# Where the float64 weight pieces of a second MoE are converted: eight or twelve of sixteen during the first MoE

## The chip, the cores and the metric
One core of a Trainium2 chip. The metric is the device time of one execution in microseconds (us); the kernel of before has a median of 831.95 us over 3 runs (831.78 to 834.63).

## What is computed
Attention with a banded mask, then a top-1 mixture of experts (first MoE), then a dense feed-forward with softplus (second MoE). What matters here:

```
# first MoE, N = 2304 tokens, D = 512, 8 experts, F = 1024
for e in range(8):
    h = np.maximum(x[mask_e] @ w1[e], 0.0)
    out[mask_e] = gate_w[mask_e] * eom[mask_e, e] * (h @ w2[e])
# second MoE
h = x @ w_in                                           # 512 x 2048
g = np.maximum(h, 0.0) + np.log1p(np.exp(-np.abs(h)))
out = g @ w_out                                        # 2048 x 512
```

`w_in` and `w_out` arrive as float64. The engines here compute in float32, so the kernel loads the 64-bit words and puts each float32 together from their two halves with shifts and masks.

## The kernel before
**Numbers.** Every product is taken in three matmuls (`mm3`, L836): each float32 operand is split into a high part (a cast, on ScalarE) and a low part (a subtraction), and hi x hi, hi x lo and lo x hi are summed in PSUM. A weight piece is 128 x 1024 numbers, 512 KB. `hi_` (L1008) casts a piece on ScalarE (L756), `lo_` (L1011) subtracts (L701) on VectorE or on GpSimd: in the first MoE the odd pieces go to GpSimd, in the second all pieces from 8 on.

**First MoE.** The loop at L1266 goes over eight experts in order of load, called ranks, with 424 columns (tokens) in rank 0 down to 256 in rank 7 (`CAPS`, L36). A rank has 16 units `u` of twelve matmuls: units 0 to 7 are `up` (L845), 8 to 15 `down` (L868). `up` writes one of three PSUM buffers (`ph`); ScalarE's ReLU (hh, L852) and VectorE (hl, L853) read it, and only then is it free. In an even unit one piece is cast, in the odd unit after it its low part is subtracted: units 0 to 7 do pieces 4 to 7 of the rank itself, units 8 to 15 pieces 0 to 3 of the next. So piece 5 is cast in unit 2 and subtracted from unit 3, piece 7 in units 6 and 7. The next rank's tokens are transposed on TensorE in units 7, 8 and 9 (L824), with two PSUM buffers (`px`); ScalarE (xh) and VectorE (xl, L701 with px as input) read them one and two units later. The third transposition therefore waits for the first xl. Engines take their instructions in the order of the program; GpSimd's order alone is left to the scheduler.

**Conversion ahead of time (prep).** `PREP` (L146) lists the tiles of 128 x 512 float64 numbers that are converted during the first MoE: 16 of them make the eight pieces below `DIRECT` (L144). `prep_tick` (L191) runs in units 0, 5, 10 and 15 of every rank from 1 on (L1311) until the list is done. One tick finishes a tile (`prep_move`: three VectorE operations at L170, L172 and L174, then a store of 256 KB to HBM on SP's queue), loads a tile four ahead (512 KB, SP's queue), and starts the next (`prep_abs` on ScalarE, L160, `prep_clamp` on VectorE, L164). The ready pieces are loaded back later like other weights (L743). All weights pass through `RB` = 5 buffers (L25); `load_next` (L992) is called when a low part is done, so that a load stands five pieces ahead of its cast.

**Second MoE.** Six blocks of 384 tokens by 16 parts of the hidden layer make 96 steps (L1398), the first 32 of them alternating between two blocks, so that the 16 pieces are needed one after another: pieces 8 to 11 from step 16 on, 12 to 15 from step 24 on. A step is twelve matmuls of `gemm1` (pg, L839 to L841) and nine of `gemm2` (q, L1378 to L1380), which lags three steps (`LAG`, L1400); the first three steps are `gemm1` alone. Softplus is made of three functions (L1342 to L1364): ScalarE's Abs, Exp, Ln (L1355) and ReLU and the cast gh (L1364), VectorE's L1349, L1351, L1356, L1358 and the low part gl (L701). In a step they come in the order c of two steps ago, a of this one, b of the last. The first two of three matmuls of `gemm2` read gh, the third (L1380) reads gl.

**Conversion in place (direct).** Pieces from `DIRECT` on are loaded as float64 in two halves (L726) and converted by `direct` (L765) in four parts at steps `D_AT + D_STEP * (j - DIRECT) + D_OFF`: Abs of each half on ScalarE; eight VectorE operations, set between those of softplus by `aside` (L760); two casts of half a piece (L785); and two half subtractions on GpSimd. `N_HL` (L29) gives the units at which ready pieces are cast, counted from rank 7's start: 16 is step 0 of the second MoE. The subtraction comes one unit later.

Of the kernel before, what the change touches and what calls it, by code (L numbers as in the profile page):

```python
# [25 lines left out]
WARM = 28  # L26
NE_AT = ((6, 14), (7, 0), (7, 1), (7, 2))
X2_AT, X2_HL = (0, 3), ((4, 5, 6, 7), (10, 11, 12, 13))
N_HL = (3, 5, 7, 9, 11, 13, 15, 16)  # L29

D_AT, D_STEP, D_OFF = 2, 3, (0, 1, 3, 4)
XG = 6
IDX_AT, GATHER_AT = 8, 12
TR_AT = (5, 7, 8, 9)
# [6 lines left out]
def attn_moe_softplus_kernel(ctx: ExitStack, tc: tile.TileContext, q, k, v, w_gate, w_ogate, w1, w2, w_in, w_out, out, dbg=None):  # L41
# [99 lines left out]
    PC = 512  # L141


    DIRECT = 8  # L144
    N_IN, N_OUT = DIRECT // 4, DIRECT // 4 * (PC // P)
    PREP = [(0, r_, c_) for r_ in range(DM // P) for c_ in range(N_IN)] + [(1, r_, 0) for r_ in range(N_OUT)]  # L146
    NPREP = len(PREP)
# [557 lines left out]
    def load_idx(r, row0, n):  # L705
        nt = (n + P - 1) // P
        t = K["ixe" if r == 0 else "ix"].tile([P, nt, 2], I32, name=f"idx{r}")
        (nc.gpsimd if r == 0 else nc.sync).dma_start(t, idx_dram[ds(row0, nt * P)].rearrange("(t p) c -> p t c", p=P))
        idx[r] = t
# [6 lines left out]
    def load_piece(r, j, e=None):  # L716
        if r == NE and j >= DIRECT:

            pieces[r, j] = []
            for h in range(2):  # L720
                if j % 2 == 0:
                    src = w_in.bitcast(I32)[256 * h : 256 * h + 256, 256 * j : 256 * j + 512].rearrange("(c p) f -> p c f", p=P)
                else:
                    src = w_out.bitcast(I32)[128 * (j - 1 + h) : 128 * (j - 1 + h) + 128].unsqueeze(1)
                t = K["wr"].tile([P, 1024], F32, tag="wr", name=f"wr{r}_{j}{h}").bitcast(I32)
                nc.sync.dma_start(t.rearrange("p (c f) -> p c f", c=src.shape[1]), src)  # L726
                pieces[r, j].append(t)
            return
        if r == NE:
            g = j // 2  # L730
            if j % 2 == 0:
                src = w_in32[:, 256 * g : 256 * g + 256].rearrange("(c p) f -> p c f", p=P)
            else:
                src = w_out32[256 * g : 256 * g + 256].rearrange("(c p) d -> p c d", p=P)
        elif j < 4:
            src = w1[ds(e, 1), :, 256 * j : 256 * j + 256].rearrange("o (c p) f -> p (o c) f", p=P)
        else:
            src = w2[ds(e, 1), 256 * (j - 4) : 256 * (j - 3)].rearrange("o (c p) d -> p (o c) d", p=P)
        if r == "v" or r == NE and j < 4:
            raw_ = K["wa"].tile([P, 1024], F32R, tag="wa", name=f"wr{r}_{j}").bitcast(F32)  # L740
        else:
            raw_ = K["wr"].tile([P, 1024], F32, tag="wr", name=f"wr{r}_{j}")
        nc.sync.dma_start(raw_.rearrange("p (c f) -> p c f", c=src.shape[1]), src)  # L743
        pieces[r, j] = [raw_]
# [55 lines left out]
    def ntile(n):  # L800
        return (n + P - 1) // P

    def gather(r, n, t):
        rows = min(P, n - P * t)
        xg[r, t] = x_ = K["xge" if r == 0 else "xg"].tile([P, DM], F32, tag="xg", name=f"xg{r}_{t}")
        return nc.gpsimd.indirect_dma_start(
            out=x_[:rows],
            out_offset=None,
            in_=x_dram[: NL0 if r == 0 else NT],
            in_offset=IndirectOffsetOnAxis(ap=idx[r][:rows, t, 0:1], axis=0),  # L810
        )
# [174 lines left out]
    def tab_load(eng, i, m):  # L986
        return eng.value_load(tabi[0:1, i : i + 1], min_val=0, max_val=m)
# [4 lines left out]
    def load_next():  # L992

        nload[1] += 1
        while nload[1] and nload[0] < len(order_):
            r, j = order_[nload[0]]
            two = r == NE and j >= DIRECT
            if two and nload[1] < 2:
                break
            if r not in er and r != NE:  # L1000
                if not K.get("ranked"):
                    break
                er[r] = tab_load(nc.sync, r, NE - 1)
            load_piece(r, j, er.get(r))
            nload[0] += 1
            nload[1] -= 1 + two
# [219 lines left out]
    def x2_load(b):  # L1226
        for h in range(2):
            if b < 2:
                t = new_b("x2r", 2 * b + h).bitcast(F32)[:, : 2 * BT]
            else:  # L1230
                t = K["wr"].tile([P, 1024], F32, tag="wr", name=f"x2r{b}{h}")[:, : 2 * BT]
            x2[b, h] = t = t.rearrange("p (c t) -> p c t", c=2)
            ld = nc.sync.dma_start(t, yT_dram[256 * h : 256 * h + 256, BT * b : BT * b + BT].rearrange("(c p) t -> p c t", p=P))


            begin = [0] + [NP // NE + (r - 1) * ((NT - NP // NE) // (NE - 1)) for r in range(1, NE)]
            need = max(r for r in range(NE) if begin[r] < BT * (b + 1))
            x2_read.append((need, ld))
            for o in range(2 * h, 2 * h + 2):
                tc.add_manual_dep(  # L1240
                    ld.ins,
                    ywr[need, o].ins.name,
                    mybir.DependencyInfo(mybir.DependencyClass.Sync, mybir.DependencyReason.DATA),
                    reason="the last rank whose columns may be read",
                )
                for r in range(need + 1, NE):
                    if (r, o) in ywr:
                        tc.declare_no_dep(ld.ins, ywr[r, o].ins, reason="later ranks lie behind these columns")
# [10 lines left out]

    for j, u in enumerate(N_HL):  # L1260
        last_rank.setdefault(u, []).append((hi_, NE, j))
# [4 lines left out]
    for r in range(NE):  # L1266
        n = CAPS[r]
        if r == 1:
            sched.close()
            overflow()  # L1270
            mctx.enter_context(tc.manual_schedule(engines=manual))
        off = tab_load(nc.scalar, NE + r, NT) if r else 0
        perm_off = tab_load(nc.sync, NE + r, NT) if r else 0
        nc.sync.dma_start(perm_dram[ds(perm_off, NT)], idx_dram[ds(er[r] * NT, NT)])
        for u in range(16):

            if r == 0:
                next(ordering, 0)
                if u == 4:
                    K["ranked"] = True  # L1280
                    er[1] = tab_load(nc.sync, 1, NE - 1)
                    load_idx(1, er[1] * NT, CAPS[1])
                    nload[1] -= 1
                    load_next()
            if r + 2 < NE:
                if u == IDX_AT:
                    if r + 2 not in er:
                        er[r + 2] = tab_load(nc.sync, r + 2, NE - 1)
                    load_idx(r + 2, er[r + 2] * NT, CAPS[r + 2])
                if 0 <= u - GATHER_AT < ntile(CAPS[r + 2]):  # L1290
                    gather(r + 2, CAPS[r + 2], u - GATHER_AT)
            if r + 1 < NE:
                m = CAPS[r + 1]
                if r == 0 and 0 <= u - 6 < ntile(m):
                    gather(r + 1, m, u - 6)
                for s, fn in zip((9, 10, 11, 12) if r == 0 else TR_AT, (gather_scale, gather_tr, gather_hi, gather_lo)):
                    if 0 <= u - s < ntile(m):
                        fn(r + 1, m, u - s)

            if r < NE - 1 or u < 8:  # L1300
                k_ = (r, 4 + u // 2) if u < 8 else (r + 1, (u - 8) // 2)
                (hi_, lo_)[u % 2](*k_)
            if r == NE - 1:
                for fn, *a in last_rank.get(u, ()):
                    fn(*a)
            if (r, u) in NE_AT:
                load_piece(NE, NE_AT.index((r, u)))
            if r == NE - 1:
                if u in X2_AT:
                    x2_load(X2_AT.index(u))  # L1310
            if r and u % 5 == 0:  # L1311
                prep_tick(new_b, NPREP, 3)
            if u < 8:
                up(r, n, u)
            else:
                down(r, n, (u - 8) // 2, u % 2, off, nc.scalar)
# [93 lines left out]
    for b in range(2, NB):  # L1410
        s0 = NF * (b - 1)
        x2_at(b, *((s0 + 8, s0 + 12, s0 + 13, s0 + 13, s0 + 14) if b == 2 else (s0 + 4, s0 + 8, s0 + 9, s0 + 10, s0 + 11)))
    for j in range(DIRECT, NF):
        for s in range(4):
            post.setdefault(D_AT + D_STEP * (j - DIRECT) + D_OFF[s], []).append((direct, j, s))
    for i in range(len(steps) + LAG):
# [54 lines left out]
```

## Time and profile before

| | |
|---|---|
| median of 3 runs | 831.95 us (831.78 to 834.63) |
| the profiled execution | 839.03 us |
| its span, first to last instruction | 837.5 us |
| mean granted TensorE clock | 0.981 |
| TensorE matmul, busy | 784.0 us (94%) |
| VectorE, busy | 551.9 us (66%) |
| ScalarE, busy | 473.7 us (57%) |
| GpSimd, busy | 199.7 us (24%) |
| DMA moved | 104.17 MB |

Attention lies ahead of 173.5 us, the first MoE between 173.5 and 420.8 us, the second from 420.8 us on. A row in order of time gives the start in us, the duration in us, the engine, the line, the operation with output <- input and shapes, and in brackets the idle time before it with what ended it. PE is TensorE, DVE VectorE, ACT ScalarE, POOL GpSimd. Matmuls overlap, so a matmul's duration is longer than the distance to the next; distances between starts are what counts.

### The profile page before, as it was taken

To read this page: it belongs to the slowest core of one execution; us is meant where nothing else is said; L and a number is where in the kernel's file an instruction comes from. 1 tells how busy PE (TensorE), PEld (TensorE's weight loads), DVE (VectorE), ACT (ScalarE), POOL (GpSimd) and SP (SyncE) were. 2 spreads that over 40 slices of the span, in tenths; PEclk is the share of its full clock that TensorE was granted. 3 is DMA by queue.
4 is the path that set the end of the run, shared out by engine and by line. 5 is a ranking of instruction groups with operands and counts; after the bars stand their busy time and mean duration, and the time that the engine had idled before them with its cause. 6 is when DMAs were issued, how large, how long until landed. Compare 5 with 4: busy or idle time off the path is not lost.

```text
span 837.5 us, 14769 instructions
## 1 busy us (share of the span) xinstructions
PE 784.0 (94%) x5542; PEld 701.9 (84%) x5543; DVE 551.9 (66%) x1079; ACT 473.7 (57%) x912; POOL 199.7 (24%) x173
## 2 busy tenths in 40 slices
PE   6788877799999999999899999999999999999995
PEld 5566645599999999999898878899999999999994
DVE  5467757474366776743778989886656665666653
ACT  3575633354546556655667566665655655655553
POOL 9501032435242454543202121211001001001001
PEclk9899989899999999999999999999999999999998
DMA  9979755418779889777832222221001001001000
GB/s 205 260 172 173 140 142 157 132 27 251 229 240 282 291 267 299 229 221 210 273 107 66 87 81 64 76 76 38 20 1 38 1 1 38 1 0 39 1 1 38
DMA packets 88844, 104.17 MB, mean 124 GB/s; under 512 B 31004, under 2 KB 65180, under 8 KB 88768
## 3 DMA queue, kind: packets, MB, share of 16 engines
q1 hardware_dynamic: 78688, 87.50, 38.3%
q0 software_dynamic: 3888, 10.12, 3.6%
q10 hardware_dynamic: 6192, 5.56, 2.0%
q8 instruction: 45, 0.74, 0.4%
q14 instruction: 31, 0.25, 0.1%
HBM read 83.98 MB, written 19.32 MB: 123 GB/s over the span
## 4 chain that ended last, share of the span: by engine, by line
PE 46%; issue 16%; DVE 6%; ACT 3%; POOL 1%; DMA 1%; SPq 0%; POOLq 0%; DVEq 0%
PE q L1380 4%; PE pg L840 4%; PE pg L841 4%; PE pg L839 4%; PE q L1378 4%; PE q L1379 4%; PE ph L839 3%; PE ph L841 3%; PE ph L840 3%; PE py L839 3%; PE py L840 3%; PE py L841 3%; DVE l L1358 1%; DVE gl L701 1%; ACT gh L1364 1%
## 5 line engine op out<-in xcount | busy, mean ns | idle before, releaser
L701 POOL TENSOR_TENSOR wl<-wr,wh 128x1024 fp32r<-128x1024 f32 (+1 forms) x46 | 99.5, 2170 | 204.0 <-ACT wh L785 108.3
L840 PE MATMUL pg<-xlm,wh 128*128 128x384 f32 x384 | 129.6, 338 | 0.0
L839 PE MATMUL pg<-xhm,wh 128*128 128x384 f32 x384 | 129.4, 337 | 0.0
L841 PE MATMUL pg<-xhm,wl 128*128 128x384 f32 x384 | 129.4, 337 | 0.0
L1380 PE MATMUL q<-wh,gl 128*128 128x512 f32 x288 | 114.0, 396 | 2.2 <-DVE gl L701 2.1
L1378 PE MATMUL q<-wh,gh 128*128 128x512 f32 x288 | 113.9, 396 | 0.4
L1379 PE MATMUL q<-wl,gh 128*128 128x512 f32 x288 | 113.1, 393 | 0.0
L1364 ACT CAST gh<-l 128x384 fp32r<-128x384 f32 x96 | 49.2, 512 | 99.9 <-DVE l L1358 99.9
L756 ACT CAST wh<-wr 128x1024 fp32r<-128x1024 f32 x72 | 75.2, 1049 | 16.2 <-ACT y L862 7.3
L701 DVE TENSOR_TENSOR gl<-l,gh 128x384 fp32r<-128x384 f32 x96 | 57.1, 595 | 41.0 <-ACT gh L1364 38.1
L839 PE MATMUL ph<-xh,wh 128*128 128x424 f32 (+7 forms) x256 | 80.7, 315 | 3.1 <-DVE hl L853 2.4
L1387 POOL DMA_INDIRECT out_dram<-o,perm_sb x18 | 18.6, 1035 | 271.9 <-DVE o L251 137.5
L839 PE MATMUL py<-hh,wh 128*128 128x424 f32 (+7 forms) x256 | 81.8, 320 | 0.0
L840 PE MATMUL py<-hl,wh 128*128 128x424 f32 (+7 forms) x256 | 80.7, 315 | 0.8 <-DVE hl L853 0.8
L841 PE MATMUL py<-hh,wl 128*128 128x424 f32 (+7 forms) x256 | 80.5, 314 | 0.0
L841 PE MATMUL ph<-xh,wl 128*128 128x424 f32 (+7 forms) x256 | 80.3, 314 | 0.0
L840 PE MATMUL ph<-xl,wh 128*128 128x424 f32 (+7 forms) x256 | 80.2, 313 | 0.0
L839 PEld LDWEIGHTS pg<-xhm,wh 128*128 128x128 f32 x384 | 72.1, 188 | 3.9
L701 DVE TENSOR_TENSOR wl<-wr,wh 128x1024 fp32r<-128x1024 f32 x42 | 61.9, 1478 | 20.4 <-ACT wh L756 14.1
L840 PEld LDWEIGHTS pg<-xlm,wh 128*128 128x128 f32 x384 | 72.1, 188 | 3.9
L841 PEld LDWEIGHTS pg<-xhm,wl 128*128 128x128 f32 x384 | 72.1, 188 | 0.0
L1349 DVE TENSOR_SCALAR w<-u 128x384 f32<-128x384 f32 x96 | 34.7, 362 | 56.4 <-ACT u L1347 55.6
(193 smaller groups left out, 1656.0 us busy)
## 6 DMA issues: line engine op xcount, KB each, us to landing
wr<-in_moe_w_dram SPq DMA_DIRECT2D x64, 512.0 KB
raw<-in_q_dram SPq DMA_DIRECT2D x8, 576.0 KB
raw<-in_k_dram SPq DMA_DIRECT2D x8, 576.0 KB
x2r<-yT_dram SPq DMA_DIRECT2D x12, 384.0 KB
vP<-in_v_dram SPq DMA_DIRECT2D x16, 272.0 KB
praw<-in_moe_w_in_dram SPq DMA_DIRECT2D x8, 512.0 KB
praw<-in_moe_w_out_dram SPq DMA_DIRECT2D x8, 512.0 KB
wr<-in_moe_w_in_dram SPq DMA_DIRECT2D x8, 512.0 KB
```

The source lines that it names most:

```text
L701: e.tensor_tensor(lo, src, hi.bitcast(F32), ALU.subtract)
L756: (eng or nc.scalar.copy)(d[1], d[0])
L839: nc.tensor.matmul(ps, wh, xh, start=(first and i == 0), stop=False)
L840: nc.tensor.matmul(ps, wh, xl, start=False, stop=False)
L841: nc.tensor.matmul(ps, wl, xh, start=False, stop=(last and i == k - 1))
L1349: nc.vector.tensor_scalar(w_, u, 1.0, None, ALU.add)
L1358: nc.vector.tensor_tensor(l, l, u, ALU.subtract)
L1364: nc.scalar.copy(gT[b, f][0], l)
L1378: nc.tensor.matmul(acc[b, t], gh[:, ts_], wh, start=(f == 0), stop=False)
L1379: nc.tensor.matmul(acc[b, t], gh[:, ts_], wl, start=False, stop=False)
L1380: nc.tensor.matmul(acc[b, t], gl[:, ts_], wh, start=False, stop=(f == NF - 1))
L1387: sc = nc.gpsimd.indirect_dma_start(out=out, out_offset=IndirectOffsetOnAxis(ap=perm_sb[:, b * (BT // P) + t, 0:1], axis=0), in_=o, in_off ...
```

## The change
Twelve pieces instead of eight are converted during the first MoE (24 tiles instead of 16), with five ticks in a rank, in units 0, 3, 6, 9 and 13. Pieces 8 to 11 become ready pieces, cast in units 18, 21, 24 and 27, which are steps 2, 5, 8 and 11 of the second MoE, and subtracted on GpSimd one step later. The four pieces 12 to 15 are still converted in place, the first at step 4, five steps apart.

```
-N_HL = (3, 5, 7, 9, 11, 13, 15, 16)
+N_HL = (3, 5, 7, 9, 11, 13, 15, 16, 18, 21, 24, 27)

-D_AT, D_STEP, D_OFF = 2, 3, (0, 1, 3, 4)
+D_AT, D_STEP, D_OFF = 4, 5, (0, 1, 3, 4)
...
-    DIRECT = 8
+    DIRECT = 12
     N_IN, N_OUT = DIRECT // 4, DIRECT // 4 * (PC // P)
...
-            if r and u % 5 == 0:
+            if r and u in (0, 3, 6, 9, 13):
                 prep_tick(new_b, NPREP, 3)
```

## Rows read from the trace of the kernel before

**Rows 1.** The table by stretch: rank 3, rank 4, and the second MoE with conversions.
```profile
core 0: us, PE busy (x) PEld busy (x) DVE busy (x) ACT busy (x) POOL busy (x), PEclk, DMA share, GB/s
281.00:311.30 30.30, 30.30 (x206) 30.01 (x205) 21.95 (x32) 18.36 (x30) 13.01 (x8) 1.00 0.92 289
311.30:340.30 29.00, 29.00 (x205) 28.77 (x204) 21.14 (x33) 18.10 (x30) 14.26 (x8) 1.00 0.87 281
...
455.00:545.00 90.00, 87.41 (x420) 73.69 (x419) 80.91 (x150) 60.47 (x130) 20.30 (x14) 1.00 0.26 75
```

**Rows 2.** TensorE in order of time, second MoE (start us, us, operation).
```profile
429.65 0.39 PE L1380 MATMUL q<-wh,gl 128*128 128x512 f32 x1
...
431.28 0.34 PE L839 MATMUL pg<-xhm,wh 128*128 128x384 f32 x1
...
443.88 0.34 PE L839 MATMUL pg<-xhm,wh 128*128 128x384 f32 x1
...
470.38 0.34 PE L839 MATMUL pg<-xhm,wh 128*128 128x384 f32 x1
...
537.94 0.34 PE L839 MATMUL pg<-xhm,wh 128*128 128x384 f32 x1
```

**Rows 3.** VectorE in order of time, second MoE.
```profile
427.76 0.56 DVE L1358 TENSOR_TENSOR l<-l,u 128x384 f32<-128x384 f32 x1
428.89 0.56 DVE L701 TENSOR_TENSOR gl<-l,gh 128x384 fp32r<-128x384 f32 x1 [0.58 <-ACT gh L1364]
...
432.44 0.56 DVE L701 TENSOR_TENSOR gl<-l,gh 128x384 fp32r<-128x384 f32 x1 [0.58 <-ACT gh L1364]
...
443.40 1.67 DVE L1358 TENSOR_TENSOR l<-l,u 128x384 f32<-128x384 f32 x1
```

**Rows 4.** ScalarE in order of time, second MoE.
```profile
426.54 0.51 ACT L1355 ACTIVATE w<-w 128x384 f32<-128x384 f32 x1
```

**Rows 5.** GpSimd in order of time, second MoE.
```profile
443.34 2.90 POOL L701 TENSOR_TENSOR wl<-wr,wh 128x512 fp32r<-128x512 f32 x2 [34.02 <-ACT wh L785]
```

**Rows 6.** Groups by line and shape, VectorE, 420.8 to 545 us.
```profile
L172 DVE SCALAR_TENSOR_TENSOR wr<-wr,cm 128x512 int32<-128x512 int32 x16 | 10.9, 683 | 0.0
...
L164 DVE TENSOR_SCALAR cm<-cm 128x512 f32<-128x512 f32 x16 | 6.7, 418 | 0.0
```

**Rows 7.** The page, part 5: costliest groups, the casts of weight pieces.
```profile
L756 ACT CAST wh<-wr 128x1024 fp32r<-128x1024 f32 x72 | 75.2, 1049 | 16.2 <-ACT y L862 7.3
```

**Rows 8.** GpSimd in order of time, ranks 3 and 5 of the first MoE.
```profile
294.03 2.62 POOL L701 TENSOR_TENSOR wl<-wr,wh 128x1024 fp32r<-128x1024 f32 x1 [5.06 <-ACT wh L756]
...
305.88 2.42 POOL L701 TENSOR_TENSOR wl<-wr,wh 128x1024 fp32r<-128x1024 f32 x1
...
345.21 2.97 POOL L701 TENSOR_TENSOR wl<-wr,wh 128x1024 fp32r<-128x1024 f32 x1 [3.35 <-ACT wh L756]
352.08 2.47 POOL L701 TENSOR_TENSOR wl<-wr,wh 128x1024 fp32r<-128x1024 f32 x1 [3.91 <-ACT wh L756]
```

**Rows 9.** VectorE in order of time, ranks 3 and 4 of the first MoE.
```profile
291.05 1.22 DVE L701 TENSOR_TENSOR wl<-wr,wh 128x1024 fp32r<-128x1024 f32 x1
...
294.31 0.90 DVE L853 SCALAR_TENSOR_TENSOR hl<-ph,hh 128x328 fp32r<-128x328 f32 x2
...
296.96 0.69 DVE L701 TENSOR_TENSOR xl<-px,xh 128x512 fp32r<-128x512 f32 x1
...
306.16 3.24 DVE L701 TENSOR_TENSOR wl<-wr,wh 128x1024 fp32r<-128x1024 f32 x1 [2.06 <-issue]
...
339.98 2.17 DVE L164 TENSOR_SCALAR pw<-pw 128x512 f32<-128x512 f32 x1 [0.57 <-ACT pw L160]
```

**Rows 10.** TensorE in order of time, ranks 3 and 5 of the first MoE.
```profile
298.14 0.45 PE L824 MATMUL px<-identf,xg 56*128 56x56 f32 x4
...
349.85 0.29 PE L839 MATMUL ph<-xh,wh 128*128 128x288 f32 x1
...
355.59 0.42 PE L824 MATMUL px<-identf,xg 24*128 24x24 f32 x4
```

## The prediction, made before the change was run

> **What bounds it.** First I read the table by stretch, to see which engine is full where. In ranks 3 and 4 of the first MoE TensorE is busy throughout and its granted clock is 1.00, the 2.4 GHz level; where the second MoE converts pieces (455 to 545 us) it is busy 87.41 of 90 us, and VectorE there 80.91 [rows 1]. So two questions decide: what this stretch loses, and whether the ranks, which lose nothing to VectorE now, stay so.
>
> Second, the matmuls by time. Three undisturbed steps take 443.88 - 431.28 = 12.60 us, 4.20 each. Between 470.38 and 537.94 lie fifteen steps, 13.51 per three [rows 2]: each piece, three steps apart, makes TensorE wait 0.91 us. Seven pieces pay that and the first about half: 7.5 x 0.91 = **6.8 us**, all that the second MoE has to give.
>
> Third, the softplus operations by time, for the cause. In an undisturbed stretch one gl follows the other by 432.44 - 428.89 = 3.55 us [rows 3]: ScalarE and VectorE run a loop that is 0.65 us shorter than a step. A piece therefore adds 13.51 - 3 x 3.55 = 2.86 us to the loop, against 1.95 that three steps have to spare. Part of that are its eight VectorE operations (0.42 to 0.68 us each [rows 6]). The rest is GpSimd: its two half subtractions run from 443.34 [rows 5], and the VectorE operation that starts at 443.40 takes 1.67 us in place of 0.56 [rows 3]. A VectorE operation on SBUF waits until the GpSimd subtraction ends. The first MoE shows it for a whole piece: GpSimd starts at 305.88, VectorE's own subtraction, 1.22 us when free as at 291.05, takes from 306.16 to 309.40 [rows 8, 9], so it began at about 308.15 and was held for **2.27 us** from GpSimd's start. The clamp, one of the operations of a tick, is held as well (2.17 us at 339.98 [rows 9], 0.42 when free [rows 6]).
>
> **The change, second MoE.** Removed: pieces 8 to 11 as direct conversions, 4 x 2.86 us of loop. The other four stand five steps apart: 5 x 0.65 = 3.25 us to spare against 2.86, so by themselves they cost nothing. Added: pieces 8 to 11 as ready ones, a cast on ScalarE and a subtraction on GpSimd each, at steps 2/3, 5/6, 8/9 and 11/12. The cast takes 1.05 us [rows 7] and fits between Ln, which ends at 426.54 + 0.51 = 427.05 [rows 4], and the next gh, which waits for L1358 to end at 428.32 [rows 3]: nothing. The subtraction is not free. Ready at 428.1, it starts when that L1358 ends, 428.32, and holds VectorE to 430.6; gl, due at 428.89, comes **1.7 us late**. The first matmul that reads gl stands at 429.65, and gl ends at 429.45 [rows 2, 3]: 0.2 us of margin, because the four opening steps are shorter than the loop.
>
> Sum over steps 3 to 13: four subtractions 4 x 1.7 = 6.8, two direct pieces (12 and 13) 5.7, together 12.5 us; to spare are 0.2 + 10 x 0.65 = 6.7. TensorE waits **5.8 us**, in place of 6.8: a gain of 1.0. The price of a whole subtraction beside the loop has no row: if VectorE's idle 0.4 us ahead of its next operation absorbs part, 1.3 each, the waits are 4.2; if a whole hold lands on the loop, 2.27 each, 8.1. So the second MoE gives between -2.6 and +1.3 us; I take -1.0, as the hold falls right before gl.
>
> **The change, first MoE.** Eight more tiles are prepared: eight loads, eight Abs on ScalarE, 8 x 4 VectorE operations (2.2 us a tick), eight stores, and later four loads of ready pieces for eight half loads of raw ones. By count the work reaches the first unit of rank 6 instead of rank 5's second tick. VectorE has room in sum (21.95 of 30.3 us in rank 3 [rows 1]); the place is what costs. The tick of unit 5 stood ahead of the GpSimd subtraction of piece 7; the tick of unit 6 meets it in every rank, since its cast is issued in unit 6. In rank 3 that subtraction starts at 294.03 [rows 8]; whichever goes first, hold, last move and clamp must all pass before the two hl behind them: 294.03 + 2.27 + 0.69 + 0.42 = 297.4. Then two hl (0.90) and xl (0.69) [rows 9], overlapping by 0.1: 298.9. The third transposition, which needs the PSUM buffer that this xl reads, stands at 298.14 [rows 10]: TensorE waits **0.8 us**. Rank 5, with units 12% shorter: 352.08 + 3.38 + 1.4 = 356.85 against 355.59 [rows 8, 10], 1.25. On this line ranks 1, 2 and 4 give 0.4, 0.6 and 1.0; in all 4.05.
>
> The tick of unit 3 meets the subtraction of piece 5 where units are short. In rank 5 that ends at 345.21 + 2.97 = 348.18 [rows 8]; two moves, clamp and hl follow, 0.69 + 0.69 + 0.42 + 0.45 less 0.1 of overlap, to 350.3, and unit 6, which needs the PSUM buffer, stands at 349.85 [rows 10]: 0.5 us. If the first, shifting operation is held too, 0.9. With half as much in rank 4, 0.75 to 1.35; I take 1.1, nearer the held end, since the clamp, of the same kind and length, is held. The Trainium skill says the same of the operation that no row shows: by SBUF — State Buffer, Who interferes with whom, a one-input VectorE operation of this kind can take both ports and is then locked out by GpSimd for a whole instruction; by that the wait would be 1.35. First MoE: **+5.15 us**.
>
> What hides the rest: the Abs goes into ScalarE's idle time (18.36 of 30.3 us busy in rank 3 [rows 1]). SP's stores wait for the last move and stand ahead of weight loads, but those run five buffers ahead, and the casts' idle time ends with ScalarE's own work, not with a load [rows 7]; without that cover each late move would be a late cast. DMA is the tight one. Rank 4 moved 281 GB/s x 29.0 us = 8.15 MB at a share of 0.87, which is 323 GB/s at full share [rows 1]; by the count it gets three loads (512 KB) and one store (256 KB) more, some 1.83 MB, and needs 30.9 us, 1.9 over. Bounds 0 and 1.9; I take 0, as the ranks lengthen by 1 to 2 us themselves. The Trainium skill, DMA: Bandwidth & Descriptors, Specifications, gives about 358 GB/s for a core's HBM; by that the estimate is 27.9 us and no loss at all.
>
> Sum: +5.15 - 1.0 = +4.15, on the profiled execution 839.03 to 843.2, on the median 831.95 to **836.1 us**. The profiled one is 0.9% above the median and used for differences only.
>
> **Rivals.** 1, faster: the holds miss. If GpSimd's subtractions in the second MoE fall into gaps of VectorE, or gl has more margin than 0.2 us, and the ticks cost 1 us in all, the 6.8 us go and the time is 826.2. For it: no rank has a wait on VectorE today. Against: the cast fixes the phase of the hold, at each of the four pieces alike. 2, slower: at the start of ranks 5 and 6 VectorE is still at the tick of the unit before (rank 6 gets one for the first time) and GpSimd's piece 5 is ready first; then VectorE's own subtraction of piece 4 and the hl behind it wait a full hold, 2.27 us a rank, 840.6. It decides when piece 5's cast ends before VectorE reaches piece 4. 3: the DMA excess of rank 4 delays weights by 1.9 us: 838.0. 4: the moved work is hidden (first MoE +0.5) and the second keeps its 5.8 us of waits: 831.5. That the change doesn't do what it says I see no way for: the counts follow from the constants.
>
> **Numbers.** My forecast has 0.50, rival 1 0.20, rival 2 0.16, rival 3 0.06, rival 4 0.08. A measurement here tells about 0.5% (4.16 us) from no change, and the forecast lies on that line: half of it counts as slower, half as the same. Slower: 0.25 + 0.16 + 0.04 = 0.45; faster: 0.17 of rival 1; same: 0.38. The range runs from rival 1 to rival 2 with the DMA excess: 826 to 842; the forecast's own is 833 to 839.
>
> **What would show it.** Right: VectorE's gl at about 430.6 behind a GpSimd subtraction and a wait near 1.5 us of TensorE at step 3; no waits after step 14; in ranks 2 to 5 a wait of TensorE for VectorE's xl ahead of the third transposition, longer in later ranks. Wrong: 4.2 us steps throughout from 431 on; ranks 1 to 6 as long as now; a ScalarE cast waiting for a load.

## The result, and the profile after

The changed kernel has a median of 843.77 us (840.34 to 848.83, 4 runs) against 833.29 us (831.78 to 835.34, 4 runs) for the kernel before: a ratio of 1.0133, 95% interval [1.0088, 1.0177]. It is slower, as the prediction had it as likeliest, but by 10.5 us in place of 4, and lies above the range (826 to 842).

The profiled execution took 848.83 us, its span is 847.3 us, 9.8 more than before. The stages split that by the starts of their first matmuls. The first MoE takes 431.09 - 172.66 = 258.43 us, **11.1 more**; the second 416.2 us to the end of the span, 0.5 less; what lies ahead of them 0.8 less.

The table by stretch, after: ranks 2 to 6 of the first MoE, then the whole second MoE (columns as in [rows 1]).
```profile
250.29:282.18 31.89, 31.50 (x206) 31.18 (x205) 27.58 (x36) 19.18 (x31) 11.99 (x8) 1.00 0.92 297
282.18:315.14 32.96, 30.87 (x206) 29.98 (x205) 28.68 (x36) 19.02 (x31) 13.40 (x8) 1.00 0.92 300
315.14:347.21 32.07, 29.57 (x206) 28.84 (x205) 27.95 (x36) 18.67 (x31) 12.48 (x8) 1.00 0.86 281
347.21:377.93 30.72, 27.44 (x206) 26.70 (x205) 26.95 (x38) 18.30 (x31) 12.42 (x7) 1.00 0.82 275
377.93:403.47 25.54, 25.54 (x202) 25.54 (x201) 12.89 (x18) 14.79 (x24) 9.88 (x5) 1.00 0.76 224
431.09:847.30 416.21, 403.74 (x2018) 364.68 (x2016) 281.12 (x531) 242.99 (x519) 40.22 (x30) 0.99 0.11 33
```
Rank 3 took 30.30 us with TensorE idle in none of them [rows 1]; now it takes 32.96 with 2.1 us idle, and VectorE's share rises from 21.95 of 30.30 to 28.68 of 32.96. The granted clock is 1.00 in all of these ranks, so the loss is waiting and not pace. Rank 6, where the work has ended, has no wait at all.

For whom TensorE waits is in the groups by line of the first MoE (173.5:420.8 before, 172.66:431.09 after; the last column is the idle time ahead of the group and what ended it). Before:
```profile
L839 PE MATMUL ph<-xh,wh 128*128 128x424 f32 (+7 forms) x256 | 80.7, 315 | 3.1 <-DVE hl L853 2.4 <-PEq L1192 0.5 <-issue 0.2
L824 PE MATMUL px<-identf,xg 128*128 128x128 f32 (+6 forms) x84 | 11.6, 259 | 0.6 <-issue 0.4 <-DVE xl L701 0.2
```
After:
```profile
L839 PE MATMUL ph<-xh,wh 128*128 128x424 f32 (+7 forms) x256 | 81.8, 320 | 8.0 <-DVE hl L853 7.3 <-PEq L1192 0.4 <-issue 0.2
L824 PE MATMUL px<-identf,xg 128*128 128x128 f32 (+6 forms) x84 | 11.7, 261 | 4.4 <-DVE xl L701 4.2 <-ACT xg L815 0.2
```
Two waits, then: 4.0 us more for xl (the third transposition) and 4.9 more for hl (a PSUM buffer of `up`). By distances between matmul starts, less the usual distance, the first is 1.36, 0.62, 0.59, 0.81 and 1.24 us in ranks 1 to 5, together 4.6; the second stands ahead of units 3 and 4 of ranks 3, 4 and 5, 1.89, 1.91 and 2.44, together 6.2. The two make 10.8 of the 11.1 us.

**The wait for hl**, at the start of rank 4 (315.14 us). VectorE, GpSimd and TensorE in order of time, after:
```profile
310.06 3.33 DVE L701 TENSOR_TENSOR wl<-wr,wh 128x1024 fp32r<-128x1024 f32 x1 [3.91 <-ACT wh L756]
313.31 0.41 DVE L170 TENSOR_SCALAR pw<-pw 128x512 int32<-128x512 int32 x1
313.76 2.92 DVE L172 SCALAR_TENSOR_TENSOR pw<-praw,pw 128x512 int32<-128x512 int32 x1
...
319.57 0.42 DVE L164 TENSOR_SCALAR pw<-pw 128x512 f32<-128x512 f32 x1
...
320.30 3.42 DVE L701 TENSOR_TENSOR wl<-wr,wh 128x1024 fp32r<-128x1024 f32 x1
323.65 0.86 DVE L853 SCALAR_TENSOR_TENSOR hl<-ph,hh 128x312 fp32r<-128x312 f32 x2
```
```profile
309.87 2.43 POOL L701 TENSOR_TENSOR wl<-wr,wh 128x1024 fp32r<-128x1024 f32 x1
313.73 2.40 POOL L701 TENSOR_TENSOR wl<-wr,wh 128x1024 fp32r<-128x1024 f32 x1 [1.44 <-ACT wh L756]
320.26 2.38 POOL L701 TENSOR_TENSOR wl<-wr,wh 128x1024 fp32r<-128x1024 f32 x1 [4.13 <-ACT wh L756]
```
```profile
324.17 0.41 PE L839 MATMUL ph<-xh,wh 128*128 128x312 f32 x1 [1.75 <-DVE hl L853]
```
Read it from the top. GpSimd's piece 1 (309.87) holds VectorE's piece 2; the tick of unit 13 comes behind it and runs into GpSimd's piece 3 (313.73: the move at 313.76 takes 2.92 us in place of 0.69). The tick of unit 0 follows without a pause until 319.99, and one hl behind it. So VectorE comes to piece 4 at 320.30, when GpSimd has taken piece 5 at 320.26: 0.04 us too late, and a whole hold. In the kernel before, the same two instructions stood the other way round, by 0.19 us:
```profile
310.50 2.78 DVE L174 SCALAR_TENSOR_TENSOR pw<-praw,pw 128x512 int32<-128x512 int32 x1
...
316.18 1.21 DVE L701 TENSOR_TENSOR wl<-wr,wh 128x1024 fp32r<-128x1024 f32 x1
```
```profile
309.92 2.81 POOL L701 TENSOR_TENSOR wl<-wr,wh 128x1024 fp32r<-128x1024 f32 x1 [1.61 <-ACT wh L756]
316.37 3.29 POOL L701 TENSOR_TENSOR wl<-wr,wh 128x1024 fp32r<-128x1024 f32 x1 [3.64 <-ACT wh L756]
```
The chain itself is therefore not new: there too piece 3 (309.92) holds the last tick of the rank before (310.50), with the tick of unit 0 behind it. What is new is when VectorE comes out of it. Counted from the rank's first matmul, GpSimd starts piece 5 of rank 4 after 5.12 us in both kernels, and VectorE comes to piece 4 after 4.93 us before and 5.16 after. In ranks 3 and 5 it was 0.73 and 0.52 us ahead of GpSimd, and is now 0.35 and 0.55 behind.

**The wait for xl**, later in the same rank, after: the tick of unit 6, whose last move is held by GpSimd's piece 7, and behind it two hl and xl.
```profile
330.03 2.90 DVE L174 SCALAR_TENSOR_TENSOR pw<-praw,pw 128x512 int32<-128x512 int32 x1
...
333.97 0.67 DVE L701 TENSOR_TENSOR xl<-px,xh 128x512 fp32r<-128x512 f32 x1
```
```profile
330.00 2.38 POOL L701 TENSOR_TENSOR wl<-wr,wh 128x1024 fp32r<-128x1024 f32 x1 [7.36 <-ACT wh L756]
```
```profile
334.70 0.43 PE L824 MATMUL px<-identf,xg 32*128 32x32 f32 x4 [0.74 <-DVE xl L701]
```

**The second MoE** keeps its waits in other places. Distances between steps of 4.20 us grow at steps 3, 9, 10, 12 and 13 by 1.46, 0.50, 1.06, 2.98 and 0.88: 6.9 us, where the kernel before lost 6.7; from step 15 on there are none. The first and the longest, after:
```profile
438.35 2.48 POOL L701 TENSOR_TENSOR wl<-wr,wh 128x1024 fp32r<-128x1024 f32 x1 [18.75 <-ACT wh L756]
...
480.12 2.36 POOL L701 TENSOR_TENSOR wl<-wr,wh 128x1024 fp32r<-128x1024 f32 x1 [10.91 <-ACT wh L756]
```
```profile
439.17 2.09 DVE L701 TENSOR_TENSOR gl<-l,gh 128x384 fp32r<-128x384 f32 x1 [0.58 <-ACT gh L1364]
...
480.49 2.41 DVE L701 TENSOR_TENSOR gl<-l,gh 128x384 fp32r<-128x384 f32 x1 [1.02 <-ACT gh L1364]
```
```profile
441.32 0.50 PE L1380 MATMUL q<-wh,gl 128*128 128x512 f32 x1 [1.22 <-DVE gl L701]
...
482.95 0.50 PE L1380 MATMUL q<-wh,gl 128*128 128x512 f32 x1 [1.71 <-DVE gl L701]
```
Each time gl (0.56 us when free, [rows 3]) waits for a whole GpSimd subtraction, and the third matmul of `gemm2` for gl.

### The profile page after: what moved, and what is told of

It is laid out like the page before. It is cut to its first block, busy times and chain, and to the rows that moved or that the text cites. A ratio compares the mean times of both kernels' runs of the same rounds, so it can differ in the third digit from the quotient of the medians.

```text
span 847.3 us, 14798 instructions
## 1 busy us (share of the span) xinstructions
PE 787.4 (93%) x5542; PEld 708.5 (84%) x5543; DVE 575.1 (68%) x1079; ACT 473.6 (56%) x908; POOL 196.8 (23%) x169
## 4 chain that ended last, share of the span: by engine, by line
PE 42%; DVE 11%; issue 11%; DMA 5%; ACT 3%; POOL 1%; SPq 1%; POOLq 0%; ACTq 0%; DVEq 0%
PE pg L840 6%; PE pg L841 6%; PE pg L839 6%; PE q L1380 6%; PE q L1378 6%; PE q L1379 6%; DVE pw L172 2%; DMA wr<-in_moe_w_dram 2%; PE py L839 2%; PE py L840 1%; PE py L841 1%; DVE wl L701 1%; DVE hl L853 1%; ACT wh L756 1%; DVE gl L701 1%
## 5 line engine op out<-in xcount | busy, mean ns | idle before, releaser
L701 POOL TENSOR_TENSOR wl<-wr,wh 128x1024 fp32r<-128x1024 f32 (+1 forms) x42 | 96.9, 2314 | 187.9 <-ACT wh L756 133.2
L701 DVE TENSOR_TENSOR gl<-l,gh 128x384 fp32r<-128x384 f32 x96 | 60.6, 631 | 46.4 <-ACT gh L1364 45.6
L756 ACT CAST wh<-wr 128x1024 fp32r<-128x1024 f32 x76 | 79.4, 1048 | 14.5 <-ACT y L862 7.7
L701 DVE TENSOR_TENSOR wl<-wr,wh 128x1024 fp32r<-128x1024 f32 x42 | 63.8, 1522 | 28.4 <-ACT wh L756 28.4
L1349 DVE TENSOR_SCALAR w<-u 128x384 f32<-128x384 f32 x96 | 36.9, 385 | 60.3 <-ACT u L1347 59.6
```

Of the source, the lines that this page charges most:

```text
L701: e.tensor_tensor(lo, src, hi.bitcast(F32), ALU.subtract)
L756: (eng or nc.scalar.copy)(d[1], d[0])
L1349: nc.vector.tensor_scalar(w_, u, 1.0, None, ALU.add)
```

## The experiments

All runs are against the kernel before on the same chip; a ratio has its 95% interval, a run without one is a single execution. Because the first MoE starts between 163.9 and 176.3 us in these traces, whatever the kernel, the stages tell more than the totals. The table has them all (us; the first MoE from its first matmul to that of the second, the second from its first matmul to its last). "Ready" are pieces 8 to 11 of the second MoE.

| run | ticks in units | low parts moved from GpSimd to VectorE | ranks 1 to 6 | first MoE | second MoE | ratio |
|---|---|---|---|---|---|---|
| before | 0 5 10 15 (16 tiles) | | 178.5 | 247.3 | 408.2 | 1 |
| after | 0 3 6 9 13 | | 190.2 | 258.4 | 407.7 | 1.0133 |
| e1 | 0 3 6 9 13 (16 tiles) | | 185.9 | 255.4 | 408.1 | 1.0051 [1.0028, 1.0074] |
| e2 | 0 3 6 9 13 | 5 | 187.1 | 255.6 | 406.9 | 1.0110 [1.0069, 1.0152] |
| e3 | 0 3 6 9 13 | 7 | 184.9 | 251.9 | 407.7 | 1.0082 [1.0048, 1.0116] |
| e4 | 0 3 6 9 13 | ready | 189.9 | 258.4 | 402.2 | 1.0092 [1.0055, 1.0128] |
| e5 | 0 3 6 9 13 | 5, 7, ready | 183.2 | 251.5 | 402.2 | 0.9982 [0.9959, 1.0006] |
| e6 | 0 5 10 12 15 | | 189.6 | 258.4 | 407.7 | |
| e7 | 0 5 10 12 15 | ready | 188.2 | 257.0 | 402.2 | 1.0041 [1.0012, 1.0070] |
| e8 | 0 3 5 9 13 | | 188.0 | 256.1 | 406.9 | |
| e9 | 0 5 10 15 | ready | 185.9 | 260.1 | 402.3 | 1.0041 [1.0012, 1.0069] |
| e10 | 0 4 8 12 | ready | 190.2 | 257.5 | 402.2 | 1.0073 [1.0038, 1.0108] |
| e11 | 0 4 10 13 | ready | 185.1 | 256.6 | 402.2 | |
| e12 | 0 5 10 15 | 7, ready | 183.0 | 254.2 | 402.2 | |
| e13 | 0 4 10 13 | 3, ready | 178.5 | 247.8 | 402.2 | 0.9888 [0.9846, 0.9930] |
| e14 | 0 4 10 12 | ready | 178.5 | 247.8 | 402.2 | |
| e15 | 0 5 10 15 | 3, 7, ready | 179.0 | 250.0 | 402.2 | |
| e16 | 0 4 10 13 | 3, 5, ready | 178.7 | 247.4 | 402.2 | 0.9926 [0.9897, 0.9955] |
| e17 | 0 4 10 12 | | 178.8 | 248.9 | 406.9 | 0.9989 [0.9965, 1.0013] |
| e18 | 0 4 10 12 | ready, and 12 to 15 | 178.5 | 247.9 | 402.0 | 0.9932 [0.9900, 0.9964] |

### One part at a time (e1 to e4)
e1, the kernel before with the changed kernel's ticks and nothing else:
```
-            if r and u % 5 == 0:
+            if r and u in (0, 3, 6, 9, 13):
```


> The kernel of before (8 pieces, 16 tiles prepared) with only the ticks moved to units 0, 3, 6, 9 and 13; the second MoE is untouched. Theory (the places of the ticks cost, through GpSimd holding VectorE): the 16 tiles end in rank 4, so ranks 1 to 4 pay most of what they pay after the change (1.5 + 0.6 + 2.7 + 3.0 us longer than before); 3 to 8 us slower than before, with TensorE waiting for xl ahead of the third transposition in ranks 1 to 4. Rival (the amount: 6 MB more DMA, eight more conversions): this run moves and converts what the kernel of before does, so it is as fast as before within 2 us.

The places, with five ticks in a rank in place of four, cost 8.1 us in the first MoE, with the same number of tiles, transfers and instructions. Ranks 3 and 4 wait for hl and ranks 1 to 3 for xl, as in the changed kernel. (Some 1.6 us of it are clock: rank 4 was granted 0.95, and behind its wait 13 matmuls in a row started at twice their usual distance.) What the four more pieces add is that the waits go on into rank 5.

e2 and e3, the changed kernel with piece 5, or piece 7, subtracted on VectorE:
```
-        on_pool = (j > 4 and j % 2 if r == 0 else j % 2 == 1) if r != NE else j >= 8
+        on_pool = (j > 4 and j % 2 if r == 0 else j in (1, 3, 7)) if r != NE else j >= 8
```
```
-        on_pool = (j > 4 and j % 2 if r == 0 else j % 2 == 1) if r != NE else j >= 8
+        on_pool = (j > 4 and j % 2 if r == 0 else j in (1, 3, 5)) if r != NE else j >= 8
```


> The changed kernel with the low part of piece 5 of ranks 1 to 7 computed on VectorE in place of GpSimd. Theory (in ranks 3 to 5 GpSimd's piece 5 goes ahead of VectorE's piece 4 and holds it 2.2 us, so hl comes late and TensorE waits for a PSUM buffer in units 3 and 4, 1.8 to 2.6 us a rank): those waits vanish, although VectorE gets 1.2 us more work a rank; 4 to 6 us faster than the changed kernel where that had all three waits. Rival (VectorE is simply full): 1.2 us more work a rank makes it 0 to 5 us slower than the changed kernel.

> The changed kernel with the low part of piece 7 of ranks 1 to 7 on VectorE in place of GpSimd. Theory (the tick of unit 6 meets GpSimd's piece 7, a hold of 2.27 us stands ahead of hl and xl): 1.2 us of VectorE work replaces the hold, and the waits ahead of the third transposition fall from 4.6 us in sum to 1 to 2; 2.5 to 3.5 us faster than the changed kernel. Rival (the tick's own 2.2 us are too many at this place): the waits stay at 4 us or grow; 0 to 2 us slower.

Without piece 5 on GpSimd the 1.9 us at units 3 and 4 of ranks 3 and 4 are all but gone (0.37 and 0), but the third transposition waits up to 1.6 us longer than before, since VectorE now has that subtraction ahead of the tick: 2.9 us gained in all, less than the 4 to 6 expected. Rank 5 gains nothing: without the hold VectorE comes to piece 4 only 6.05 us after the rank's first matmul, 0.6 later than in the changed kernel, and unit 3 waits 1.4 us. So piece 5's hold is not the whole of the loss there. Without piece 7 the third transposition's waits go from 4.6 us to 0.4, which shows that hold as their cause, and the first MoE gains 6.5, twice what was expected; those at units 3 and 4 are gone in rank 3 and stay in ranks 4 and 5.

e4, the ready pieces' low parts on VectorE:
```
-        on_pool = (j > 4 and j % 2 if r == 0 else j % 2 == 1) if r != NE else j >= 8
+        on_pool = (j > 4 and j % 2 if r == 0 else j % 2 == 1) if r != NE else False
```


> The changed kernel with the low parts of pieces 8 to 11 in the second MoE on VectorE in place of GpSimd. Theory (each whole subtraction on GpSimd holds VectorE right ahead of gl for 1.7 us): 1.2 us of VectorE work that is in order with the loop replaces it, and the second MoE's waits fall from about 7 us to 1; it then takes 410 to 411 us from its first matmul to the end, in place of 416.2, and the kernel is 5 to 6 us faster than the changed one. Rival (the wait comes from VectorE's load, whoever subtracts): the second MoE stays at 415 to 418 us.

The second MoE loses its waits but for 1.4 us at steps 13 and 14, 407.7 to 402.2 us; step 3 is 4.17 us long. The group of matmuls that read gl, second MoE, after (431:847) and then e4 (423.37:840):
```profile
L1380 PE MATMUL q<-wh,gl 128*128 128x512 f32 x288 | 113.4, 394 | 3.2 <-DVE gl L701 3.2
```
```profile
L1380 PE MATMUL q<-wh,gl 128*128 128x512 f32 x288 | 112.9, 392 | 0.2 <-DVE gl L701 0.2
```
The 1.22 us that VectorE takes for a piece, in its own place in the order, cost less than the 2.4 us of GpSimd that lock it out.

### Together, and at other places (e5 to e8)
e5 is e2, e3 and e4 in one:
```
+        on_pool = (j > 4 and j % 2 if r == 0 else j in (1, 3)) if r != NE else False
```


> The changed kernel with the low parts of pieces 5 and 7 (ranks 1 to 7) and of pieces 8 to 11 on VectorE, e2, e3 and e4 together: no GpSimd subtraction is left beside units 0 to 8 of a rank, nor beside the second MoE's ready pieces. Theory (the holds are the cost, not the amount of work): the first MoE's eight ranks take 249 to 252 us (changed kernel 258.4, before 247.3), the second MoE's matmuls 402 to 403 us (407.7, before 408.2), and the kernel is 2 to 5 us faster than the one of before. Rival (VectorE full): with 2.4 us more a rank the waits ahead of the third transposition grow, the first MoE stays at 255 us or more, and the kernel is not faster than before.

No difference from the kernel before that can be told: the second MoE keeps its 6 us, but the first is still 4.2 us longer. With all that work on VectorE ranks 4 and 5 wait 1.5 and 2.5 us.

e6 keeps the old units and adds unit 12; e7 is e6 with the ready low parts on VectorE:
```
-            if r and u in (0, 3, 6, 9, 13):
+            if r and u in (0, 5, 10, 12, 15):
```


> The changed kernel with the ticks in units 0, 5, 10, 12 and 15: the four places of before and one in unit 12, where VectorE was idle for about 2 us. Theory (the places cost, not the amount): no wait ahead of the third transposition beyond what the kernel of before has; the waits at the start of ranks 3 to 5 depend on which of two subtractions comes first by 0.2 us or less, so 0 to 6 us there; the first MoE takes 247 to 254 us (258.4 in the changed kernel). Rival (a fifth tick a rank fills VectorE and DMA, wherever it is): 256 to 260 us.

> e6 and e4 together: ticks in units 0, 5, 10, 12 and 15, and the low parts of pieces 8 to 11 on VectorE. Theory: first MoE as in e6 (247 to 254 us), second MoE's matmuls 402 to 403 us; between 6 us faster than before and 1 us slower, according to the waits at the start of the ranks. Rival (work moved into the first MoE always costs there what the second saves): 830 to 834 us, no difference from before.

Ranks 1 to 3 are as before to 0.1 us, the transposition does not wait up to rank 4, but ranks 5 and 6 lose 4.0 to 5.4 us, mostly at units 3 and 4. I put that down to ticks 10, 12, 15 and 0 following each other too closely for short units, which no run shows by itself. The first MoE came out at 258.4 and 257.0 us, where the rival of e6 had it (256 to 260), but with ranks 1 to 3 free and not "wherever it is".

e8 moves the tick of unit 6 to unit 5:
```
-            if r and u in (0, 3, 6, 9, 13):
+            if r and u in (0, 3, 5, 9, 13):
```


> The changed kernel with one tick a rank moved, from unit 6 to unit 5. Theory (the tick of unit 6 meets GpSimd's piece 7): one unit earlier the tick's last operations are through when GpSimd starts, as in the kernel of before; the waits ahead of the third transposition fall from 4.6 us in sum to under 1.5. The waits at the start of ranks 3 to 5 stay. Rival (the tick itself is late, whatever GpSimd does): behind piece 6's own low part it is even later, and the waits stay at 4 us or more.

The third transposition still waits 0.4 to 1.7 us longer than before: behind the tick of unit 3 that of unit 5 is late itself, and in rank 4 its clamp still runs into GpSimd's piece 7 (2.62 us at 326.35). So it is not unit 6 as such. 2.3 us fewer in all.

### Four ticks in a rank (e9 to e12)
24 tiles at four in a rank reach to the start of rank 7. All four have the ready low parts on VectorE (as e4); e12 has piece 7 there too.
```
-            if r and u in (0, 3, 6, 9, 13):
+            if r and u % 5 == 0:                 # e9, e12
+            if r and u in (0, 4, 8, 12):         # e10
+            if r and u in (0, 4, 10, 13):        # e11
```


> All 24 tiles, but at the four units of before (0, 5, 10, 15), so that the work reaches through ranks 5 and 6; and the ready pieces' low parts on VectorE. Theory (the places cost, not the amount): ranks 1 to 4 within 0.5 us of before (35.5, 31.3, 30.3, 29.1); ranks 5 and 6, where units 15 and 0 follow each other closely and units are short, each 0 to 4 us longer than in before (26.8 and 25.5); second MoE 402.2 us against 408.2. In all 0.99 to 1.003 of before. Rival (the amount costs: eight more tiles on VectorE, GpSimd and DMA, wherever they stand): ranks 1 to 6 together some 8 us longer, no gain in all.

> As the run with the old units, but in units 0, 4, 8 and 12, which lie between GpSimd's subtractions (started in units 2, 6, 10 and 14) and never follow each other closely. Theory: ranks 1 to 6 within 1 us each of before, no waits at units 3 and 4, at most small waits at unit 9 since the tick of unit 8 stands ahead of xl; first MoE 247 to 251 us, second 402.2, 0.988 to 0.996 of before. Rival (any place costs where VectorE has four ticks a rank and short units): ranks 5 and 6 together over 5 us longer.

> As the run before it, but units 10 and 13 in place of 8 and 12, so that no tick stands at the transpositions. Theory: no waits at unit 9; but the tick of unit 10 meets GpSimd's piece of that unit, as in before, without a wait there; first MoE 247 to 250 us, second 402.2. Rival (the tick of unit 13 backs VectorE up into the next rank's start): 0.5 to 2 us at units 3 and 4 of ranks 3 to 6.

> The run with the old units and piece 7's low part on VectorE in place of GpSimd. Theory: nothing is gained in ranks 1 to 4, since the tick of unit 5 does not meet piece 7; VectorE gets 1.2 us a rank more just ahead of the transpositions' low parts, which costs 0 to 0.5 us in each of ranks 3 to 6. Rival (every hold of GpSimd costs something): first MoE 1 to 3 us shorter than with the old units alone.

Four misses, and each says where. e9 fell at the start of rank 4 with ticks where the kernel before has them: there 0.19 us decide, as shown above (3.7 us longer: 1.9 waited at unit 4, and a granted clock of 0.95). It lost 2.7 us in rank 6 and 5.2 in rank 7. e10 has no wait at units 3 and 4 up to rank 6, but 1.6 to 1.8 us more than before at every third transposition up to rank 5, since the tick of unit 8 stands right ahead of xl; I had put that down as small. e11 waits no longer than before at the transpositions and lost 2.4 and 4.2 us in ranks 4 and 6, at units 3 and 4 (some 1.6 of the 4.2 are clock, granted at 0.94). e12 was free up to rank 5, against what I expected of piece 7, and lost 4.5 in rank 6. The start of rank 4 in e11, VectorE and GpSimd:
```profile
302.57 2.62 DVE L170 TENSOR_SCALAR pw<-pw 128x512 int32<-128x512 int32 x1
...
309.54 3.02 DVE L701 TENSOR_TENSOR wl<-wr,wh 128x1024 fp32r<-128x1024 f32 x1
```
```profile
302.36 2.54 POOL L701 TENSOR_TENSOR wl<-wr,wh 128x1024 fp32r<-128x1024 f32 x1 [0.81 <-ACT wh L756]
309.02 2.45 POOL L701 TENSOR_TENSOR wl<-wr,wh 128x1024 fp32r<-128x1024 f32 x1 [4.12 <-ACT wh L756]
```
The same chain as in the changed kernel: the tick of unit 13 held by piece 3, the tick of unit 0 behind it, then piece 5 goes ahead of piece 4.

### What makes VectorE late (e13 to e16)
```
+            if r and u in (0, 4, 10, 13):        # e13, e16
+            if r and u in (0, 4, 10, 12):        # e14
+            if r and u % 5 == 0:                 # e15
+        on_pool = (... else j in (1, 5, 7)) if r != NE else False     # e13
+        on_pool = (... else j in (1, 5)) if r != NE else False        # e15
+        on_pool = (... else j in (1, 7)) if r != NE else False        # e16
```


> Ticks 0, 4, 10, 13, ready low parts on VectorE, and piece 3 of the next rank (units 14 and 15) on VectorE in place of GpSimd. Theory (GpSimd's piece 3 holds VectorE's last tick by 2.3 us, so that it comes too late for piece 4): VectorE does 1.2 us more but is 1 us earlier at the next rank's start; ranks 4 and 6 as in before (29.1, 25.5; they were 31.5 and 29.7), first MoE 248 to 251 us. Rival (the tick of unit 13 as such is too much): ranks 4 and 6 over 1.5 us longer than before.

> Ticks 0, 4, 10 and 12, pieces as in the run with 0, 4, 10 and 13. Rival (the last tick stands too late): ranks 4 and 6 as in before, first MoE 248 to 251 us. Theory (GpSimd's piece 3 holds whatever VectorE does then): the tick is over before piece 3, so also free, but unit 10 is held by piece 1 and unit 12 follows it closely; ranks 4 and 6 between 0 and 2 us longer than before.

> Ticks 0, 5, 10, 15 with pieces 3 and 7 on VectorE (the run before had piece 7 there alone, rank 6 at 30.1 us). Theory: without piece 3's hold the tick of unit 15 ends some 1 us earlier and rank 6 is 25.5 to 27.5 us; first MoE 249 to 252. Rival (units 15 and 0 are too close in short ranks, hold or not): rank 6 stays at 29 to 30 us.

> Ticks 0, 4, 10, 13 with pieces 3 and 5 on VectorE: neither hold is left near a rank's start. Theory: no waits at units 3 and 4 of any rank up to 6, first MoE 247 to 250 us, second 402.2 us; in all 0.988 to 0.995 of before. Rival (VectorE gets too full, as where all low parts were on it): 0.5 to 2.5 us each in ranks 4 to 6.

Piece 3 off GpSimd (e13) frees ranks 4 and 6 (29.09 and 25.54 us). So does the last tick one unit earlier (e14), where piece 3 still holds VectorE (2.62 us at L170) but there is time for it: VectorE comes to piece 4 1.1 us ahead of GpSimd's piece 5. It is neither the hold nor the tick alone, then, but how late the two together leave VectorE. At the old units, too, piece 3 was what kept rank 6 long: 30.05 us in e12, 25.96 in e15. Piece 5 on VectorE as well as piece 3 (e16) adds nothing: its rank 6 is 0.2 us longer than e13's. The start of rank 4 in e13, and its table row:
```profile
301.75 1.22 DVE L701 TENSOR_TENSOR wl<-wr,wh 128x1024 fp32r<-128x1024 f32 x1
...
305.40 1.22 DVE L701 TENSOR_TENSOR wl<-wr,wh 128x1024 fp32r<-128x1024 f32 x1
```
```profile
306.19 2.70 POOL L701 TENSOR_TENSOR wl<-wr,wh 128x1024 fp32r<-128x1024 f32 x1 [7.58 <-ACT wh L756]
```
```profile
301.07:330.16 29.09, 29.09 (x206) 28.86 (x205) 23.35 (x35) 18.02 (x30) 10.38 (x6) 1.00 0.93 311
```
Piece 4 starts 0.79 us ahead of piece 5. **All 24 tiles are prepared and the first MoE is within 0.5 us of the one before**, and with 402.2 us in the second the kernel beats the one before on the same chip: 822.42 us against 830.64, 0.9888 [0.9846, 0.9930]. By the stages it is 5.5 us (0.7%).

### The change with other places only, and GpSimd out of the second MoE (e17, e18)
e17 is the changed kernel with its ticks in units 0, 4, 10 and 12 and nothing else; e18 is e14 with the direct pieces' halves on VectorE:
```
-                sub(nc.gpsimd, d[3][:, hs[h]], w_[h], d[2][:, hs[h]])
+                sub(nc.vector, d[3][:, hs[h]], w_[h], d[2][:, hs[h]])
```


> The change as it is, with its ticks moved to units 0, 4, 10 and 12 and nothing else. Theory (the places of the ticks are the whole loss in the first MoE): first MoE 247 to 249 us in place of 258.4, second 406.5 to 408 as in the change; in all the same as before, 0.995 to 1.003. Rival (GpSimd's ready pieces or the extra loads cost the first MoE something too): first MoE over 250 us.

> Ticks 0, 4, 10, 12, ready low parts on VectorE, and the half subtractions of the four direct pieces on VectorE too, so that GpSimd subtracts nothing in the second MoE. Theory (what is left there, 0.5 and 1.0 us at steps 13 and 14, is GpSimd's hold): second MoE 400.7 to 401.5 us in place of 402.2. Rival (VectorE is full where a direct piece is converted; each half adds 0.6 to 0.7 us to it): 402.2 to 404 us. In all 0.985 to 0.995 of before.

e17 shows that the ticks' places are the loss, and not the amount of work. It has four ticks in a rank in place of five, so their number changes with their places: at 0, 5, 10 and 15 or 0, 4, 8 and 12 four a rank lost about as much (e9, e10), and no run found five a rank to be free (e5, without the holds of pieces 5 and 7, still lost 4.7 us in ranks 3 to 5). With the ticks moved, the change costs the first MoE 1.6 us (0.9 of it in rank 7, at a load), gives 1.3 in the second, and is 0.9989 [0.9965, 1.0013], the same as before. e18 gained 0.2 us in the second MoE, between the two expectations. It still waits 1.1 us at step 13 with no GpSimd subtraction there, against 0.5 and 1.0 at steps 13 and 14 in e14. As the halves are now VectorE's own work, the run does not tell how much of e14's waits was the hold.

## Why the prediction was wrong
- **Failed step: "The tick of unit 3 meets the subtraction of piece 5 ... I take 1.1."** No unit 6 waited, so the 1.1 us were not there. The cost came earlier, from the start of the rank, and was 6.2 us. It is rival 2's mechanism, given 0.16, by the condition it named: piece 5's cast ends before VectorE reaches piece 4. But it was in three ranks, 3 to 5 and not 5 and 6, at 1.9 to 2.4 us each (2.27 priced). I followed the new ticks of units 3 and 6 and the end of the work, and put rival 2 down to units getting short; the tick of unit 13 was not followed past GpSimd's piece 3 into the next rank. Before, rank 4 had 0.19 us to spare there; that margin was in the trace and was not looked at, and VectorE came 0.23 us later. e2 shows the hold as the cause in ranks 3 and 4, e11 against e13 and e14 what makes VectorE late; in rank 5 VectorE is late without the hold too.
- **The third transposition** was right in place and in sum: 0.4, 0.6, 0.8, 1.0, 1.25 expected in ranks 1 to 5, 1.36, 0.62, 0.59, 0.81, 1.24 measured; 4.05 against 4.6. Rank 1 is no steady figure: e4, whose first MoE is the same program, has 0.20 there. e3 shows the cause, e8 that another unit alone does not mend it.
- **The second MoE**: -1.0 expected, -0.5 measured. Step 3 came 1.46 us late (1.5 expected), with gl behind a GpSimd subtraction. The waits are 6.9 in place of 5.8, the longest at step 12. In e2, e8 and e17, whose second MoE is the same program, they are 6.1, and it takes 1.3 less than before; the changed kernel's 0.8 more stands at steps 12 to 14, where its granted clock was 0.92. So the size was right within what executions differ by. Rival 1's condition, that the holds miss, did not come about. e4 shows the cause.
- **DMA**: nothing, as taken. e13's rank 4 moved 311 GB/s x 29.09 us = 9.05 MB at a share of 0.93 without a wait of TensorE, so the 1.9 us of rival 3 were no bound here. The amount was counted too high: the changed kernel's rank 4 moved 281 x 32.07 = 9.0 MB, 0.9 more than before in place of 1.83.
- **The operation that no row had shown** is held: L170 took 2.62 us in e11 behind GpSimd at 302.36, 0.41 when free. The Trainium skill, SBUF — State Buffer, Who interferes with whom, says that `tensor_scalar` can take VectorE's two ports, of which it shares the second with GpSimd, and that whichever of the two issues first then blocks the other for the whole instruction. The trace agrees: 2.2 us of GpSimd's 2.54. The unit 6 that this was to delay did not wait all the same.
- The sum with the measured terms: 4.6 + 6.2 - 0.5 = 10.3 us, by which the profiled 839.03 becomes 849.3 (848.83 measured). Rival 2's 840.6 had the size of the hold right and one rank too few, and dropped none of the forecast's other terms, the 1.1 us at unit 6 among them; the range, which ends at rival 2 and the DMA excess, was too short by that rank. (That end adds up to 842.5 and the hold, by its rows, to 2.30; neither matters here.)

## What to carry to other kernels
Work put on an engine that has room on average costs what stands behind it in that engine's order: follow each inserted block to the next meeting with an engine that locks it out, also across the border of a loop's pass, and read the margin there before costing anything (0.19 us decided some 2 us a rank here). Try the same work at other places before giving it up: 24 tiles cost 11 us in units 0, 3, 6, 9 and 13 and 0.5 to 1.6 us in 0, 4, 10 and 12. Where VectorE bounds a loop, a subtraction of 1.2 us in its own order can cost less than the same one on an idle GpSimd, which holds VectorE for 2.3 (e4).

## What the hardware showed
- Which of two engines goes first was settled by 0.04 us (after) and 0.19 us (before), and a whole subtraction hung on it each time. Places near such a tie are unsafe: rank 4 took 29.09 us before and 32.78 in e9 with the same ticks up to there, and 30.37 in e6 and 29.39 in e7, whose first MoE is the same program.
- The clock after a wait: around step 12 of the second MoE, where TensorE waited 1.71 us in one piece, the granted clock was 0.92, in part at the lower level of 1.2 GHz: three matmuls of `gemm1` that otherwise take 0.52 us took 0.97 from 485.32. The table by stretch, after:
```profile
466.00:488.00 22.00, 19.28 (x85) 15.98 (x84) 18.81 (x31) 12.43 (x27) 5.57 (x3) 0.92 0.32 95
488.00:500.00 12.00, 12.00 (x61) 10.85 (x61) 9.64 (x18) 8.46 (x19) 2.91 (x2) 1.00 0.27 76
```
In the first MoE a wait of 1.91 us ahead of unit 4 left rank 4 of the changed kernel at 1.00, but went with 0.95 in rank 4 of e1 and e9, which then lost some 1.6 us more to the clock; what makes the difference no run here settles.
